# Batch 1's second product as seven block products, begun one stretch earlier

## The chip, the cores and the metric

The kernel runs on one core of one Trainium2 chip. A core has five engines that run side by side, each with its own queue of instructions in a fixed order: TensorE (PE, matrix products, results in PSUM), VectorE (DVE), ScalarE (ACT), GpSimd (POOL) and SyncE (SP, which here only issues transfers). An instruction starts when those ahead of it in its queue have been started and the semaphores that it waits for have been reached. The metric is the device time of one execution in microseconds (us); runs of the kernel before took 203.54 to 203.85 us, with a median of 203.78 over three.

## The reference

Two stages follow each other. Attention between 512 tokens and 32 state rows, for 8 batches b and 8 heads, and then a two-layer network over all rows:

```python
scores  = scale * x @ state.T        # 512 x 32 a head; softmax over the 32 -> a
xread   = a @ state                  # 512 rows a batch
scores2 = scale * state @ x.T        # 32 x 512; softmax over the 512 -> a2
sread   = a2 @ x                     # 32 rows a batch
y = concat(xread, sread)             # heads side by side: 544 rows of 512 a batch, 4352 in all
h = y @ w_in                         # 512 -> 2048
out = max(0.01 * h, h) @ w_out       # 2048 -> 512
```

Inputs and output are float32; the kernel computes its products in bfloat16 with float32 sums.

## The kernel before

**Stretches.** The work goes batch by batch. For batch b the kernel forms M = state @ w_in per head (`a_m` and `m_evict`, lines 359 to 385, in four column groups), the attention weights aT (256 rows of heads and states by 512 tokens), and then hT = leaky_relu(M.T @ aT), the hidden layer transposed: 16 tiles of 128 hidden columns by 512 tokens. A stretch is a loop of 16 steps s; step s makes tile s of hT with two products of 512 columns (`ff1`, line 389) into a PSUM bank of the tag `ph` (two banks in turn), from which ACT takes it with the leaky relu. In batch 1's stretch (the loop at line 1061) steps 6 and 10 make two tiles at once into the wide bank `big` (`ff1_pair`, line 399), and steps 7 and 11 make none. Between these steps other work is written by hand, on each engine in the order in which the code calls it: nothing is rearranged by a scheduler.

**The second product.** hT times w_out is done one batch behind. Two ways exist:
- plainly, in pieces (`piece`, line 593): piece (b, i, jq) adds four products of 512 columns for row group i (128 tokens) into a bank of the tag `py`, for a quarter jq of the hidden layer; after jq = 3 the bank is copied to `ysb` and stored.
- with seven block products instead of eight (Strassen's scheme in Winograd's form; `Fast`, line 638). Tokens and hidden columns are halved, and w_out is cut into four blocks B11 to B22. The operands of blocks 5, 6, 7 and 3 are sums: of hT's parts (`su0` to `su3`, DVE) and of w_out's (`tw`, four sums of 128 x 2048, made once by `weights_sum`). A block n goes in 8 units m; a unit is one product of 256 columns for each 128 tokens. Blocks run in the order 1, 2, 6, 5, 7, 3, 4 in two PSUM banks (`py`): when blocks 1, 6, 5 and 7 end, ACT copies the bank (`save`, `sv`); when 2, 3 and 4 end, DVE adds a saved copy (`join`) into `yo`, and POOL adds for block 7; then the result is stored.

Batches 2 to 7 use `Batch`: 512 tokens, so a unit is two products. Its first 15 units (`own`) run at the end of the batch's own stretch, as soon as the tiles of hT that they read are there; the other 41 in the next batch's. `PACE` says how many units each step runs. Batch 0 goes in pieces. Batch 1 is mixed: row groups 0 and 1 in pieces, of which 6 of 8 run in its own stretch (the list `fill`, odd steps 5 to 15) and two in steps 0 and 1 of batch 2's; row groups 2 and 3 as `Half`, a `Batch` of 256 tokens whose 56 units of one product run in batch 2's stretch, seven a step. `PACE2` is batch 2's own pace, used from step 10 on.

**Around it.** Batch 1's stretch also holds the last pieces of batch 0 (w_out's last quarter arrives at 34.75 us, so the pieces with jq = 3 are late: row groups 2 and 3 ahead of the loop, 0 and 1 in steps 1 and 3), batch 2's scores, their row maxima, the shift and the exponential (`a_scores`, `a_shift`, `a_exp`, `a_probs`; DVE, then ACT, then DVE), the column softmax (`a_max2`, `a_exp2`, and `a_probs2` for its factors), and the casts of batch 3's x (POOL). The sums of w_out are made in parts: half of two of them early on POOL, the rest on DVE ahead of the loop, the last one in batch 2's stretch at step 4.

## Time and profile before

| | |
|---|---|
| median of 3 runs (lowest, highest) | 203.78 us (203.54, 203.85) |
| the profiled execution, its span | 203.07 us, 201.3 us |
| busy share of PE, DVE, ACT, POOL | 96%, 78%, 72%, 24% |
| batch 1's stretch, 34.8 to 51.1 us | PE 16.2, DVE 13.7, ACT 13.6 us busy of 16.3 |
| batch 2's stretch, 51.1 to 73.6 us | PE 22.2, DVE 19.8, ACT 18.8 us busy of 22.5 |
| granted TensorE clock | 0.998 |

The profile is of one execution; times in it count from the span's start. A line of a timeline gives the start, the length, the engine, the line of the kernel, the operation, the tiles (written <- read) and their sizes, how many like it follow each other, and in brackets for how long the engine was idle before and what ended that. Lengths of PE's products overlap each other: what a product costs a busy PE is the distance from one start to the next. "The chain that ended last" follows the end of the program back through what each instruction waited for.

### The profile page before, as it was taken

The page shows a single profiled execution, that of the slowest core. Times are in us where ns is not written, and L with a number is a line of the kernel's source. Part 1 is how long each engine was busy: PE and PEld are TensorE (multiplying, and loading weights), DVE is VectorE, ACT ScalarE, POOL GpSimd, SP SyncE. Part 2 cuts the span into 40 slices and gives each one's busy share as a digit, 9 for nine tenths or more (in the row PEclk, how much of TensorE's full clock was granted, in tenths as well). Part 3 has the DMA queues.
Part 4 walks back from the last instruction along what each step waited for, and adds up shares of the span by engine and source line. Part 5 has one row for each costly group of instructions (what it writes and reads, how often), then busy time and mean ns, then how long its engine had stood idle before and what let it go on. Part 6 is the DMA issues. An engine that isn't in the chain of part 4 may idle for free.

```text
span 201.3 us, 4920 instructions
## 1 busy us (share of the span) xinstructions
PE 194.1 (96%) x2020; PEld 132.2 (66%) x2042; DVE 157.1 (78%) x242; ACT 145.3 (72%) x268; POOL 47.3 (24%) x76
## 2 busy tenths in 40 slices
PE   7899999999999999999999999999999999999993
PEld 2567633444377567766776677676766688799882
DVE  1676689798789889975997599779978977995622
ACT  3478747689869886978697868787878768767710
POOL 8841065040018004200420040200020014104250
PEclk9999999999999999999999999999999999999999
DMA  6999997999692993249433975250027101310035
GB/s 172 225 206 260 248 293 132 205 249 251 101 297 65 223 246 76 44 180 262 88 68 136 283 54 111 104 156 5 0 92 172 29 0 72 139 52 3 0 93 171
DMA packets 40758, 28.01 MB, mean 139 GB/s; under 512 B 25312, under 2 KB 37728, under 8 KB 40736
## 3 DMA queue, kind: packets, MB, share of 16 engines
q1 hardware_dynamic: 35536, 20.88, 43.0%
q0 software_dynamic: 4912, 6.55, 15.9%
q8 instruction: 16, 0.26, 0.5%
q10 hardware_dynamic: 288, 0.26, 0.5%
q14 instruction: 6, 0.05, 0.1%
HBM read 17.30 MB, written 8.91 MB: 130 GB/s over the span
## 4 chain that ended last, share of the span: by engine, by line
PE 80%; DMA 15%; POOL 2%; issue 1%; DVE 0%; POOLq 0%
PE yq L670 40%; PE ph L392 20%; DMA w_out_bf<-in_moe_w_out_dram 10%; DMA w_in_bf<-in_moe_w_in_dram 5%; PE py L599 4%; PE pf L466 3%; PE yu L670 3%; PE pm L371 3%; PE pl L555 2%; PE psn L337 1%; PE sc L211 1%; PE pyw L599 1%; PE phw L403 1%; POOL w_in_bf L123 1%; PE yz L670 0%
## 5 line engine op out<-in xcount | busy, mean ns | idle before, releaser
L397 ACT ACTIVATE hT<-ph 128x512 bf16<-128x512 f32 x100 | 58.9, 605 | 17.3 <-PE ph L392 13.1
L392 PE MATMUL ph<-aT,M 128*128 128x512 bf16 x183 | 54.9, 379 | 0.3
L670 PEld LDWEIGHTS <-su 128*128 128x128 bf16 x448 | 42.9, 98 | 13.8 <-DVE su L659 0.8
L670 PEld LDWEIGHTS <-hT 128*128 128x128 bf16 x312 | 30.1, 98 | 13.5 <-issue 2.0
L670 PE MATMUL yq<-tw_xf,su 128*128 128x256 bf16 x208 | 29.6, 273 | 0.3
L670 PE MATMUL yq<-w_out_bf,hT 128*128 128x256 bf16 x208 | 29.2, 273 | 0.1
L111 POOL CAST xb<-xl 128x512 bf16<-128x512 f32 (+1 forms) x24 | 14.3, 638 | 59.1 <-DMA xl<-in_x_dram 45.1
L392 PEld LDWEIGHTS <-M 128*128 128x128 bf16 x200 | 19.4, 98 | 7.2 <-issue 1.0
L659 DVE TENSOR_TENSOR su<-hT 128x1024 bf16<-128x1024 bf16 x26 | 17.9, 688 | 7.1 <-ACT hT L397 7.1
L740 POOL TENSOR_TENSOR yo<-sv,sv 128x512 f32<-128x512 f32 x6 | 7.8, 1302 | 41.0 <-ACT sv L679 25.4
L679 ACT COPY sv<-yq 128x512 f32<-128x512 f32 (+1 forms) x28 | 15.4, 554 | 2.1 <-PE yq L670 1.4
L599 PEld LDWEIGHTS <-hT 128*128 128x128 bf16 x96 | 9.0, 98 | 10.9 <-issue 1.3
L599 PE MATMUL py<-w_out_bf,hT 128*128 128x512 bf16 x60 | 15.4, 379 | 0.3 <-issue 0.2
L670 PE MATMUL yq<-tw_x,su 128*128 128x256 bf16 x104 | 14.6, 273 | 0.1
L670 PE MATMUL yq<-w_out_bf,su 128*128 128x256 bf16 x104 | 14.5, 273 | 0.2
L385 ACT CAST M<-pm 128x1024 bf16<-128x1024 f32 x13 | 13.2, 1014 | 0.9 <-PE pm L371 0.8
L670 PE MATMUL yq<-tw_x,hT 128*128 128x256 bf16 x96 | 13.6, 273 | 0.0
L682 DVE TENSOR_TENSOR yo<-yq,sv 128x512 f32<-128x512 f32 x17 | 11.6, 684 | 1.5 <-PE yq L670 1.5
L291 ACT ACTIVATE e<-sc,mcols 128x512 bf16<-128x512 f32 x16 | 11.0, 693 | 0.2 <-DVE mcols L285 0.2
L283 DVE TENSOR_REDUCE mcol<-sc 128x2 f32<-128x1024 f32 x8 | 9.7, 1216 | 0.0
L659 DVE TENSOR_TENSOR su<-su,hT 128x1024 bf16<-128x1024 bf16 x13 | 9.0, 692 | 0.4
L221 DVE TRANSPOSE_TENSOR_REDUCE mrow<-sc 128x32 f32<-128x1024 f32 x7 | 8.7, 1243 | 0.6 <-PE sc L211 0.5
(173 smaller groups left out, 299.0 us busy)
## 6 DMA issues: line engine op xcount, KB each, us to landing
xl<-in_x_dram SPq DMA_DIRECT2D x5, 1024.0 KB, 6.9
out_dram<-yo SPq DMA_DIRECT2D x10, 512.0 KB, 2.8
w_in_bf<-in_moe_w_in_dram POOLq DMA_DIRECT2D x4, 512.0 KB, 9.1
w_out_bf<-in_moe_w_out_dram POOLq DMA_DIRECT2D x4, 512.0 KB, 17.7
out_dram<-ysb SPq DMA_DIRECT2D x8, 256.0 KB, 5.7
xf<-in_x_dram SPq DMA_DIRECT2D x2, 512.0 KB, 5.1
x<-in_x_dram POOLq DMA_DIRECT2D x2, 512.0 KB, 14.1
xl<-in_x_dram POOLq DMA_DIRECT2D x1, 1024.0 KB, 20.4
```

Source lines behind the costliest of these rows:

```text
L111: copy(xs[b][:, :, h0:h1].rearrange("p t h d -> p h t d"), xl[b][:, h0:h1].rearrange("p h (t d) -> p h t d", t=NT),)
L221: nc.vector.tensor_reduce(out=m1[:], in_=flat.rearrange("p (c j) -> p c j", j=NS), axis=AX.X, op=ALU.max, apply_transpose=True,)
L283: nc.vector.tensor_reduce(out=m2[:], in_=a.sc[:], axis=AX.X, op=ALU.max, negate=True)
L291: nc.scalar.activation(out=a.e2[:, g], in_=a.sc[:, g, :], func=AF.Exp, bias=a.m2s[:, g:g + 1], scale=SCALE, accum_out=a.r2[:, g:g + 1],)
L385: copy(a.M[:, :, cols], pm[:])
L392: nc.tensor.matmul(ph[:], lhsT=a.M[:, g, P * j:P * (j + 1)], rhs=a.aT[:, g, :], start=(g == 0), stop=(g == 1),)
L397: nc.scalar.activation(out=hT[:, j, :], in_=ph[:], func=AF.Prelu, alpha=0.01)
L599: nc.tensor.matmul(y.py, lhsT=hT[:, j, P * i:P * (i + 1)], rhs=w_out_bf[:, j, :], start=(j == 0), stop=(j == 15),)
L659: (eng or nc.vector).tensor_tensor(out=S[n][:, ms], in0=u[:, ms], in1=v[:, ms], op=op)
L670: nc.tensor.matmul(bank[:, i, :], lhsT=lhs[:, m, P * i:P * (i + 1)], rhs=rhs[:, m, :], start=(first and m == 0 and (i == 0 or of is not No ...
L679: copy(t[:], bank)
L682: nc.vector.tensor_tensor(out=dst, in0=bank, in1=self.sv[n][:], op=ALU.add)
```

## The change

- `Half` goes. Batch 1's second product is a `Batch` of 512 tokens like the others, all seven blocks for all four row groups: 112 products of 256 columns in place of 32 of 512 and 56 of 256. Thirteen of its units run in batch 1's own stretch (`early`: 3 in step 7, then one or two a step), in an order of their own that follows the tiles of hT; 43 run in batch 2's stretch by a new `PACE2`, ahead of batch 2's 15 own ones.
- Batch 0's last pieces: only row group 2's stays ahead of the loop; row group 3's goes to step 1, 0's to step 3, 1's to step 5. The copy of row group 0's result moves from ACT to DVE.
- The sums of w_out on DVE come ahead of these copies; half of sum 0 and half of sum 3 move to POOL, ahead of its casts of batch 3's x; the other half of sum 3 comes in step 7 of batch 2's stretch.
- The factors of the column softmax (`a_probs2`) of batches 1, 2 and 3 are made together in step 11 of batch 2's stretch, behind which stands batch 1's last join; its buffer `r2` becomes three.
- In batch 2's stretch the first halves of the sums 0 and 1 come ahead of the copy of M, batch 3's scores go from step 1 to step 2, sums 2 and 3 stand in and behind the shift, the next batch's first sums go from step 12 to 13.
- On SP, batch 0's `a2T` transposition comes ahead of batch 0's four stores; batch 1's result leaves in two stores of 512 KB instead of four of 256 KB.

```diff
@@ -287,7 +287,7 @@
     def a_exp2(a, g):
         if g == 0:
             a.e2 = att.tile([P, 2, S], BF16, name="e2", tag="e2", bufs=3)
-            a.r2 = att.tile([P, 2], FP32, name="r2", tag="r2")
+            a.r2 = att.tile([P, 2], FP32, name="r2", tag="r2", bufs=3)
         nc.scalar.activation(
             out=a.e2[:, g], in_=a.sc[:, g, :], func=AF.Exp,
             bias=a.m2s[:, g:g + 1], scale=SCALE, accum_out=a.r2[:, g:g + 1],
@@ -691,7 +691,11 @@
             self.b, self.f = b, Fast(hT[:], 2 * P, [(spool, f"su{n}", 1) for n in range(4)], saved)
             self.units = [(n, m) for n in (1, 2, 6, 5, 7, 3, 4) for m in range(NM)]
             own = [(n, m) for n in (1, 2) for m in range(6)] + [(1, 6), (2, 6), (1, 7)]
-            assert len(own) == OWN
+            if b == 1:
+                own = [(n, 2 * c + m) for c in range(2) for n in (1, 2) for m in range(2)]
+                own += [(n, m) for m in (4, 5) for n in (1, 2)] + [(1, 6)]
+                self.units.sort(key=lambda u: u != (1, 7))
+            self.ahead = len(own)
             self.units = own + [u for u in self.units if u not in own]
             self.bank = {}
             self.yos = {}
@@ -749,25 +753,9 @@
                 f.join(self.yo(1)[:, :, :HC], bank, 7)
                 self.out(1)
 
-    class Half(Batch):
-
-
-        def __init__(self, hT):
-            super().__init__(1, hT)
-            self.f.__init__(hT[:, :, 2 * P:], P, self.f.homes, self.f.saved)
-            self.units = [(n, m) for n in (1, 2, 6, 5, 7, 3, 4) for m in range(NM)]
-
-        def yo(self, r):
-            if r not in self.yos:
-                self.yos[r] = ypool.tile([P, 1, DM], FP32, name="ysb", tag="ysb", bufs=3)
-            return self.yos[r]
-
-        def out(self, r, cols=slice(0, DM), i=None, eng=nc.sync):
-            eng.dma_start(rows_of(1)[2 + r], self.yo(r)[:, 0, :])
-
     OWN = 15
     PACE = (1, 4, 4, 4, 3, 4, 4, 3, 4, 4, 4, 4, 3, 4, 3, 3)
-    PACE2 = (0,) * 10 + (3, 3, 2, 2, 2, 3)
+    PACE2 = (1, 2, 1, 3, 4, 4, 4, 4, 4, 4, 4, 4, 4, 5, 5, 5)
 
     att_of = [Attn() for _ in range(B)]
     a0, a1, a2 = att_of[:3]
@@ -1043,38 +1031,43 @@
     a_probs(a1)
     for i in range(NT):
         piece(0, h0, i, 2)
-    for i in (2, 3):
-        piece(0, h0, i, 3, copy=None)
-    for i in (2, 3):
-        y_store(0, i, VEC)
+    piece(0, h0, 2, 3, copy=None)
+    for n in (2, 0, 1):
+        weights_sum(n, 4, 8)
+    weights_sum(3, 4, 8, nc.gpsimd)
+    weights_sum(0, 0, 4, nc.gpsimd)
     for h in range(0, H, 2):
         cast_x(3, h, h + 2, POO)
     a_a2t(a0)
-    weights_sum(2, 4, 8)
-    weights_sum(1, 4, 8)
-    weights_sum(0)
 
 
 
     h1 = hpool.tile([P, 16, S], BF16, name="hT", tag="hT")
-    fill = [(0, h0, 0, 3), (0, h0, 1, 3)] + [(1, h1, i, jq) for jq in range(3) for i in range(2)]
+    before = Batch(1, h1)
+    early = {7: 3, 8: 1, 9: 2, 10: 1, 11: 2, 12: 1, 13: 1, 14: 1, 15: 1}
+    assert sum(early.values()) == before.ahead
     for s in range(16):
         if s in (6, 10):
             ff1_pair(a1, h1, s, "big")
         elif s not in (7, 11):
             ff1(a1, h1, s)
-        if s % 2:
-            pb, hT, i, jq = fill[s // 2]
-            piece(pb, hT, i, jq)
+        if s == 1:
+            piece(0, h0, 3, 3, copy=None)
+            for i in (2, 3):
+                y_store(0, i, VEC)
+        elif s in (3, 5):
+            piece(0, h0, s // 2 - 1, 3, copy=VEC if s == 3 else SCA)
+        else:
+            before.run(early.get(s, 0))
         if s == 3:
             a_scores(a2)
             m_evict(a2, 0, a_m(a2, 0, "big"), SCA)
             a_shift(a2)
             a_max2(a2)
-            a_probs2(a0)
         if s == 7:
             a_exp(a2)
             a_probs(a2)
+            a_probs2(a0)
             a_open(att_of[3], 3)
             a_xt_dma(att_of[3])
         elif s in (9, 11):
@@ -1084,32 +1077,26 @@
 
 
 
-    a_probs2(a2)
     pm = [a_m(a2, 1, "big"), a_m(a2, 2, "sc")]
+    for n in (0, 1):
+        before.f.sums(n, 0, 4)
     m_evict(a2, 1, pm[0], VEC)
     m_evict(a2, 2, pm[1], SCA)
-    a_probs2(a1)
     a_a2t(a1)
 
 
 
-    before, half = None, Half(h1)
     for b in range(2, B):
         hT = hpool.tile([P, 16, S], BF16, name="hT", tag="hT")
         a = att_of[b]
         nxt = att_of[b + 1] if b + 1 < B else None
         now = Batch(b, hT)
-        std = []
-        if b == 2:
-            std = [(i, 3) for i in range(2)]
-            for n in (0, 1):
-                half.f.sums(n)
 
         def fill(s):
             units((PACE2 if b == 2 else PACE)[s])
 
         def units(n):
-            left = min(n, len(before.units)) if before else 0
+            left = min(n, len(before.units))
             if left:
                 before.run(left)
             if n > left:
@@ -1131,10 +1118,9 @@
                 if b + 2 < B:
                     load_x(b + 2, nc.sync)
                 a_a2t(a)
-                if before:
-                    for n in (0, 1):
-                        before.f.sums(n, 4, 8)
-            elif s == 1:
+                for n in (0, 1):
+                    before.f.sums(n, 4, 8)
+            elif s == (2 if b == 2 else 1):
                 if nxt is not None:
                     a_scores(nxt)
                 m_evict(a, 3, a_m(a, 3, "big"), SCA)
@@ -1143,20 +1129,23 @@
                 elif b % 2:
                     a_sread_rows([att_of[b - 2], att_of[b - 1]])
                 if b == 2:
-                    half.f.sums(2)
                     a_shift(nxt, 0)
+                    before.f.sums(2)
+                    a_shift(nxt, 1)
+                    a_max2(nxt)
+                    before.f.sums(3, 0, 4)
+                    before.f.sums(3, 4, 8)
                 elif nxt is not None:
                     a_shift(nxt)
                 if b + 2 < B:
                     open_xb(b + 2)
                     for h in range(0, H, 2):
                         cast_x(b + 2, h, h + 2, POO)
-                if before:
+                if b > 2:
                     before.f.sums(2, 4, 8)
-            elif s == 3:
-                if before:
-                    before.f.sums(3)
-                if nxt is not None and b > 2:
+            elif s == 3 and b > 2:
+                before.f.sums(3)
+                if nxt is not None:
                     a_max2(nxt)
             elif s == 4:
                 if b == 2:
@@ -1168,7 +1157,7 @@
             elif s == 8:
                 if nxt is None:
                     a_sread(a)
-            elif s == 12:
+            elif s == (13 if b == 2 else 12):
                 for n in range(3):
                     now.f.sums(n, 0, 4)
             if nxt is None:
@@ -1191,6 +1180,10 @@
                 if b == 2 and s < 11:
                     if s in (8, 9):
                         a_exp2(nxt, s - 8)
+                    elif s == 7:
+                        a_exp(nxt)
+                        weights_sum(3, 0, 4)
+                        a_probs(nxt, 0)
                 elif s == 5:
                     a_exp(nxt)
                 elif s in (7, 8):
@@ -1198,24 +1191,11 @@
                     if s == 7:
                         a_probs(nxt)
                 elif s == 11:
-                    a_probs2(nxt)
+                    for some in ((a1, a2, nxt) if b == 2 else (nxt,)):
+                        a_probs2(some)
                 elif s in (12, 13):
                     SCA(nxt.M[:, s - 12, DM:2 * DM], pm1[:, s - 12, :])
-            if std:
-                i, jq = std.pop(0)
-                piece(1, h1, i, jq)
-            elif b == 2 and half.units:
-                half.run(7)
-                if s == 4:
-                    a_shift(nxt, 1)
-                    half.f.sums(3)
-                    weights_sum(3)
-                    a_max2(nxt)
-                elif s == 6:
-                    a_exp(nxt)
-                elif s == 8:
-                    a_probs(nxt, 0)
-            elif s != 11 and not fast:
+            if s != 11 and not fast:
                 fill(s)
             if s == 10 and nxt is not None:
                 pm0 = a_m(nxt, 0, "big")
```

## The prediction

> **What bounds the kernel now.** I read the page's first part, then the chain that ended last, then the table by stretch for the two stretches that the change touches, then the timelines of TensorE (PE), ScalarE (ACT), VectorE (DVE) and GpSimd (POOL) there. The page and the chain:
>
> ```profile
> PE 194.1 (96%) x2020; PEld 132.2 (66%) x2042; DVE 157.1 (78%) x242; ACT 145.3 (72%) x268; POOL 47.3 (24%) x76
> ```
>
> ```profile
> 15.54 19.21 DMA w_out_bf<-in_moe_w_out_dram
> 34.80 1.24 PE pyw L599 x5
> ```
>
> From 34.80 us, when the last quarter of w_out has landed, the chain is PE's own work almost without a break; so in what follows time is PE's work plus PE's waits. By stretch (columns: length, busy time of each engine with instructions, granted clock, DMA):
>
> ```profile
> 34.80:51.10 16.30, 16.19 (x86) 7.00 (x87) 13.65 (x21) 13.62 (x26) 2.29 (x4) 1.00 1.07 223
> 51.10:73.60 22.50, 22.18 (x237) 13.73 (x242) 19.82 (x31) 18.80 (x36) 4.98 (x6) 1.00 0.79 184
> ```
>
> The first line is batch 1's stretch, the second batch 2's. The clock granted is 1.00. ACT and DVE are busy 13.6 of 16.3 us in the first: they follow PE closely there, and if PE's work shrinks by some 2 us, one of them can become the bound. PE's timeline (start, length, what, count) gives the prices:
>
> ```profile
> 40.07 0.41 PE L211 MATMUL sc<-xT,st_t 64*32 64x512 bf16 x8
> ...
> 51.12 0.63 PE L371 MATMUL pm<-w_in_bf,st_t 64*32 64x512 bf16 x16
> ...
> 52.12 1.03 PE L599 MATMUL py<-w_out_bf,hT 128*128 128x512 bf16 x4
> ...
> 74.22 1.05 PE L670 MATMUL yq<-tw_xf,su 128*128 128x256 bf16 x8
> ```
>
> Four 512-column products are issued in 0.86 us (the last one's end is modelled, so spacing counts, not length; 52.12 to 52.99 us), 0.2156 us each. Eight 256-column products take 0.87 us (0.109 each; the next instruction follows at 75.10). A group of scores and M products costs 0.56 (40.07 to 40.63), the pair of M products after the stretch also 0.56. DVE, ACT and POOL:
>
> ```profile
> 27.87 1.25 DVE L229 STREAM_TRANSPOSE mrowb<-mrow 128x1024 f32<-128x1024 f32 x1
> 29.15 1.22 DVE L234 TENSOR_TENSOR sh<-sc,mrowb 128x1024 f32<-128x1024 f32 x1
> ...
> 34.97 0.69 DVE L259 TENSOR_TENSOR aT<-e,qb 128x1024 bf16<-128x1024 bf16 x1
> ...
> 40.55 1.25 DVE L221 TRANSPOSE_TENSOR_REDUCE mrow<-sc 128x32 f32<-128x1024 f32 x1
> ...
> 84.63 1.05 DVE L259 TENSOR_TENSOR aT<-e,qb 128x1024 bf16<-128x1024 bf16 x1
> ```
>
> ```profile
> 44.44 1.06 ACT L241 ACTIVATE e<-sh 128x1024 bf16<-128x1024 f32 x1
> 45.40 1.06 ACT L397 ACTIVATE hT<-ph 128x512 bf16<-128x512 f32 x2
> 46.35 0.69 ACT L291 ACTIVATE e<-sc,mcols 128x512 bf16<-128x512 f32 x1
> ...
> 47.02 1.03 ACT L407 ACTIVATE hT<-phw 128x1024 bf16<-128x1024 f32 x1
> 47.92 0.70 ACT L291 ACTIVATE e<-sc,mcols 128x512 bf16<-128x512 f32 x1
> ...
> 48.58 1.11 ACT L397 ACTIVATE hT<-ph 128x512 bf16<-128x512 f32 x2
> ```
>
> ```profile
> 26.77 2.12 POOL L636 TENSOR_TENSOR tw_x<-w_out_bf 128x1024 bf16<-128x1024 bf16 x1 [10.47 <-DMA w_out_bf<-in_moe_w_out_dram]
> 28.96 2.13 POOL L636 TENSOR_TENSOR tw_xf<-w_out_bf,tw_x 128x1024 bf16<-128x1024 bf16 x1
> ...
> 43.28 2.29 POOL L111 CAST xb<-xl 128x512 bf16<-128x512 f32 x4 [9.36 <-DMA xl<-in_x_dram]
> ...
> 83.86 1.27 POOL L740 TENSOR_TENSOR yo<-sv,sv 128x512 f32<-128x512 f32 x1 [5.99 <-ACT sv L679]
> ```
>
> To be seen: DVE's shift of batch 2's scores begins at 40.55 and ACT's exponential of it at 44.44, 3.89 later; from there ACT runs without a hole to 49.7, and the relu after the second `e<-sc,mcols` starts 4.14 after the exponential. After the change ACT has these instructions in the same order.
>
> **PE's work.** Rows 0 and 1 of batch 1's second product go as 8 pieces of four 512-column products: 32 x 0.2156 = 6.90 us out. Rows 2 and 3 are 56 products of 256 columns, 6.10 us; now all four rows make 112, 12.21 us. Sum: 12.21 - 6.10 - 6.90 = -0.79 us. That is the whole gain that PE can have. In batch 1's stretch PE loses 24 of the 512s (one piece of batch 0 also moves into it from ahead of it, which is neutral) and gains 26 of the 256s: -5.17 + 2.83 = -2.34. Batch 2's stretch loses 8 of the 512s and 56 of the 256s and gains 86: -1.72 - 6.10 + 9.37 = +1.55. So the change moves work out of a stretch where ACT has 2.7 us to spare into one where PE is the only bound.
>
> **Batch 1's stretch, walked through.** PE: piece (0,2,3) from 34.80 to 35.66. The first step needs aT, which DVE writes until 35.66 (34.97 + 0.69); signal and weight load add about 0.14 (nowhere shown alone; bounds 0 and the 0.31 of a switch to small tiles, 40.07 less 39.76), so 35.80. Two steps of 0.43 and a piece to 37.52, two steps and piece (0,0,3) to 39.25; scores at about 39.35 instead of 40.07. DVE: three sums of w_out fit from 35.6 to 37.5 while PE works; two copies follow; the copy that was ACT's can begin when (0,0,3) has left PE, about 39.46, and holds DVE for 0.60. So the shift starts at 40.06, though its scores are there at 39.80: the moved copy takes 0.26 from the 0.72 gained. ACT's exponential: 40.06 + 3.89 = 43.95.
>
> PE meanwhile: 39.35 + 0.56 = 39.91, steps 4 and 5 with piece (0,1,3) to 41.63, wide step 6 to 42.50, then with 3, 1, 2, 1, 2, 1 units (0.218 each) steps 7 to 12 end at 46.84. Step 13's unit (1,5) reads hT column 10, which the wide relu writes: in the rows above it starts 2.58 after the exponential and takes 1.02, so 47.55, with signal and weight load 47.70; PE is there at 47.27 and waits 0.43. Step 14 needs the `ph` bank that step 12's relu frees: 43.95 + 4.14 + 0.60 = 48.69, about 48.73; PE is there at 47.92 and waits 0.81. Then 48.73 + 0.65 + 0.65 = 50.03, with the switch of tiles 50.12 for the M products instead of 51.12. The stretch gains 1.00 of its 2.34.
>
> Behind it: ACT has the 1.01 us M copy, a relu and the copy of block 1 in line, and batch 2's third step waits for the first relu's bank about 0.17 (PE there at 52.20, relu ended 52.33 plus 0.04). Before lost 0.12 in this stretch (68.91 to 69.03), which the fuller steps now cover.
>
> **The moves that cost nothing, and their cover.** POOL's two sums (2.12 each, 37.5 to 41.8) stand ahead of its casts, which waited for the load of x until 43.28: 1.5 us of cover. If it were gone, the casts, batch 3's xT and its scores would be late next; xT is issued at 45.6 as before. SP: batch 0's a2T now goes ahead of four 256 KB stores, two of which left earlier; nobody waits for stores, the state loads and xT behind them stand behind the cast anyway. Later two 512 KB stores replace two 256 KB ones and the two pieces' ones; batch 2's first join into the same buffer comes near 73.3, some 8 us after batch 1's store goes (a store lands in 2.8). DVE in batch 2's stretch: two more sums (1.20), one sum twice as wide (0.53), one more sum (0.61), three joins wider by 0.26 (0.78), two of the three statistics pairs come in from elsewhere (0.65), half of the last w_out sum goes (1.62 to 0.61): +2.8 us or so, against 2.7 idle (22.5 less 19.8) and 1.55 of added length. The tightest: block 3's first sum ends near 60.9, PE wants it near 62.0; its cover is 1.1 us. ACT there: two copies of 0.59 and four of 0.37 become four of 0.58, about even. Joins ahead of batch 2's sums: the last join is ready when PE ends block 4, so it delays those sums by at most its 0.60, and before batch 3's step 2 they have over 3 us.
>
> **Sum.** -0.79 + 0.14 + 0.43 + 0.81 + 0.17 - 0.12 = +0.64 us. Rounding and reading of the signal times move this by 0.15 or so; I take +0.6. The profiled execution took 203.07 us (span 201.3 and 1.8 around it); it becomes about 203.7. The median of the three runs is 203.78, 0.7 above the profiled one; on it the forecast is **204.4 us**, 0.3% slower. What this kernel's measurement can tell from no change is about 0.2%, 0.41 us.
>
> **Where a page bears on it.** The row: aT on DVE took 1.05 us at 84.63 beside a POOL add, 0.69 at 34.97 alone. The Trainium skill, "SBUF — State Buffer", section "SBUF: two separate sides", says that VectorE and GpSimd take a shared port pair as an exclusive lock and the later one "fully blocks", for a VectorE instruction with two SBUF inputs or in a two-port mode. By that rule POOL's new sums hold none of the copies and the shift, which have one SBUF input at most, and the trace agrees (27.87 and 29.15 took 1.25 and 1.22 us beside POOL's sums of 26.77 and 28.96); a lock without that condition would give the last rival.
>
> **Rivals.** (1) *ACT's debt never reaches PE, and it gets faster.* If the exponential starts early enough, PE's two waits go. Each 0.1 us of an earlier start takes 0.1 off the waits; from 43.3 on the change breaks even, at about 42.7 both are gone and the sum is near -0.6, 203.2; with the full -0.79, 203.0. For it: PE reaches the scores 0.72 earlier, and nothing in the trace of before shows PE waiting for ACT there. Against: DVE's chain of 3.89 is serial. (2) *The waits and the saving cancel:* the exponential starts near 43.4; 203.8, no change. (3) *Batch 2's stretch also waits on DVE:* from 1.1 us of lateness on, block 3 waits for its sum. DVE's +2.8 against 4.2 of room argues against it; the casts of x on POOL beside the wide sum argue for it (59.60: four took 3.73 instead of 2.29). A sum held as long as those casts (1.44) and by one cast more (0.61), less the 1.1 of cover, gives 0.9 more: 205.3. (4) *POOL's sums hold DVE's copies and shift:* each can be held up to 2.12, so up to 2.1 more on the exponential, one for one: 206 at most. The rows at 27.87 and 29.15 speak against it; a copy of PSUM beside a POOL sum is not in the trace (bounds 0 and 2.12; I take 0, the two neighbours' value).
>
> **Numbers.** Forecast 0.51 (its own range 204.0 to 204.9), rival 1 0.20, rival 2 0.12, rival 3 0.13, rival 4 0.04. Faster by over 0.2%: 0.20. Within 0.2% (203.37 to 204.19): rival 2 and the low tail of the forecast, 0.24. Slower: 0.56. The range from 203.0 to 205.3 leaves out rival 4, the tail of rival 3 and a little under rival 1.
>
> **What will show it.** Right if: no PE wait before the scores (near 39.35), the exponential near 43.95, PE waiting for ACT between 47 and 49 by 1.0 to 1.4 us in two places, the M products near 50.1, and `psn` of batch 3's stretch near 74.2 instead of 73.58. The forecast is wrong if the exponential starts before 43.3, if PE waits for DVE's `su` in batch 2's stretch, or if DVE's copies near 37.7 take over 0.9 us beside POOL.

## The result and the profile after

The changed kernel takes 204.2 us (median of eight runs, 203.74 to 204.63); the kernel before took 203.72 us on the same chip (203.53 to 203.98). The ratio is 1.0026, with a 95% interval of 1.0014 to 1.0037: slower by about 0.53 us, where the forecast was 204.4 us and a loss of 0.6. The profiled execution took 204.26 us, span 202.5; it was forecast at 203.7.

The page's first part, then the table by stretch for the two stretches (columns as before: length, busy time of PE, its weight loads, DVE, ACT, POOL, granted clock, DMA):

```profile
PE 195.2 (96%) x2066; PEld 134.3 (66%) x2066; DVE 159.9 (79%) x246; ACT 144.9 (72%) x265; POOL 51.2 (25%) x78
```

```profile
34.80:50.20 15.40, 14.35 (x91) 7.02 (x89) 14.46 (x21) 12.49 (x24) 6.48 (x6) 1.00 1.06 231
50.20:74.20 24.00, 23.99 (x254) 15.92 (x260) 22.49 (x36) 19.26 (x36) 4.57 (x6) 1.00 0.63 161
```

PE's share is 96% as before, but batch 1's stretch now has holes: 14.35 us busy of 15.4, where before it was 16.19 of 16.3. Batch 2's stretch has hardly any (23.99 of 24.0), and DVE fills 22.49 us of it (19.82 of 22.5 before). PE's timeline:

```profile
36.29 1.04 PE L392 MATMUL ph<-aT,M 128*128 128x512 bf16 x4
...
39.85 0.41 PE L211 MATMUL sc<-xT,st_t 64*32 64x512 bf16 x8
...
47.35 0.59 PE L392 MATMUL ph<-aT,M 128*128 128x512 bf16 x2
48.11 0.39 PE L670 MATMUL yq<-w_out_bf,hT 128*128 128x256 bf16 x2 [0.16 <-ACT hT L407]
49.26 0.59 PE L392 MATMUL ph<-aT,M 128*128 128x512 bf16 x2 [0.76 <-ACT hT L397]
...
50.65 0.63 PE L371 MATMUL pm<-w_in_bf,st_t 64*32 64x512 bf16 x16
...
52.30 0.60 PE L670 MATMUL yq<-w_out_bf,hT 128*128 128x256 bf16 x4
52.91 0.59 PE L392 MATMUL ph<-aT,M 128*128 128x512 bf16 x2
...
64.88 0.84 PE L371 MATMUL pm<-w_in_bf,st_t 64*32 64x512 bf16 x24
...
66.54 1.03 PE L392 MATMUL ph<-aT,M 128*128 128x512 bf16 x4
...
74.58 0.70 PE L337 MATMUL psn<-xb,a2T 128*32 128x64 bf16 x64
```

Step 13 begins at 47.35, and its unit is due 0.43 later, at 47.78; it starts at 48.11, 0.33 late. Step 14 is due 0.22 behind that unit, at 48.33, and starts at 49.26, 0.93 late. (The bracket, here 0.16 and 0.76, holds only what the profile puts down to the semaphore; it comes out 0.17 below the lateness counted this way.) Together 1.26 us. In batch 2's third step four products from 52.30 on end their issue at 52.74, and the step starts at 52.91: 0.17. ACT, DVE and POOL in the same stretch:

```profile
44.44 1.06 ACT L241 ACTIVATE e<-sh 128x1024 bf16<-128x1024 f32 x1 [0.21 <-DVE sh L234]
...
47.02 1.03 ACT L407 ACTIVATE hT<-phw 128x1024 bf16<-128x1024 f32 x1
...
48.58 1.11 ACT L397 ACTIVATE hT<-ph 128x512 bf16<-128x512 f32 x2
```

```profile
35.54 0.69 DVE L259 TENSOR_TENSOR aT<-e,qb 128x1024 bf16<-128x1024 bf16 x1
...
38.23 1.29 DVE L609 COPY ysb<-pyw 128x512 f32<-128x512 f32 x2 [0.19 <-PE pyw L599]
39.96 0.69 DVE L609 COPY ysb<-py 128x512 f32<-128x512 f32 x1 [0.44 <-PE py L599]
40.56 1.24 DVE L221 TRANSPOSE_TENSOR_REDUCE mrow<-sc 128x32 f32<-128x1024 f32 x1
...
64.73 0.18 DVE L250 TENSOR_SCALAR r<-r 128x32 f32<-128x32 f32 x1
...
65.78 0.69 DVE L1205 CAST M<-pm 128x512 bf16<-128x512 f32 x1
```

```profile
38.12 2.12 POOL L636 TENSOR_TENSOR tw_x<-tw_xf,w_out_bf 128x1024 bf16<-128x1024 bf16 x1 [3.97 <-DVE tw_xf L636]
40.20 2.12 POOL L636 TENSOR_TENSOR tw_xf<-w_out_bf 128x1024 bf16<-128x1024 bf16 x1
43.70 2.28 POOL L111 CAST xb<-xl 128x512 bf16<-128x512 f32 x4 [1.38 <-DMA xl<-in_x_dram]
```

The exponential starts at 44.44, 3.88 behind the maximum at 40.56, which had to wait for the moved copy (39.96). The wide relu starts 2.58 and the relu of step 12 4.14 behind the exponential, as before. The copies on DVE beside POOL's sum took 0.69 and, two together, 1.29 us; POOL's sums ended at 42.3, and its casts still waited 1.38 us for x. Everything in this execution is about half a microsecond later than forecast from the first step on, and the chain that ended last says why: it no longer starts with w_out's landing, but with the first load of x and DVE's work on batch 1's weights.

```profile
1.26 6.25 DMA xf<-in_x_dram
...
34.26 1.26 DVE qb L258
```

`aT` began at 35.54 here and at 34.97 in the profile of before. There it did not matter, as the first step came 0.86 after aT's end at 35.66; here the first step starts 0.06 after aT's end. The first step and batch 3's `psn` in the profile of before:

```profile
36.52 1.03 PE L392 MATMUL ph<-aT,M 128*128 128x512 bf16 x4
...
73.58 0.70 PE L337 MATMUL psn<-xb,a2T 128*32 128x64 bf16 x64
```

### The profile page after: what moved, and what is told of

The parts are those of the page before. It is cut to its first block, busy times and chain, and to the rows that moved or that the text cites. A ratio compares the mean times of both kernels' runs of the same rounds, so it can differ in the third digit from the quotient of the medians.

```text
span 202.5 us, 4991 instructions
## 1 busy us (share of the span) xinstructions
PE 195.2 (96%) x2066; PEld 134.3 (66%) x2066; DVE 159.9 (79%) x246; ACT 144.9 (72%) x265; POOL 51.2 (25%) x78
## 4 chain that ended last, share of the span: by engine, by line
PE 83%; DVE 8%; DMA 3%; ACT 3%; issue 0%; POOL 0%; SPq 0%; DVEq 0%; ACTq 0%; POOLq 0%
PE yq L670 41%; PE ph L392 20%; PE pm L371 4%; DMA xf<-in_x_dram 3%; PE pf L466 3%; PE yu L670 3%; PE ph L944 2%; PE pl L555 2%; PE py L599 1%; PE pyw L599 1%; DVE mrowb L229 1%; DVE sh L234 1%; DVE mrow L221 1%; PE sc L211 1%; PE psn L337 1%; ACT hT L397 1%
## 5 line engine op out<-in xcount | busy, mean ns | idle before, releaser
L392 PE MATMUL ph<-aT,M 128*128 128x512 bf16 x200 | 58.2, 379 | 0.9 <-ACT hT L397 0.8
L670 PEld LDWEIGHTS <-su 128*128 128x128 bf16 x480 | 45.9, 98 | 15.0 <-DVE su L659 0.8
L670 PEld LDWEIGHTS <-hT 128*128 128x128 bf16 x336 | 32.3, 98 | 15.4 <-issue 2.1
L670 PE MATMUL yq<-w_out_bf,hT 128*128 128x256 bf16 x224 | 31.7, 273 | 0.2 <-ACT hT L407 0.2
L670 PE MATMUL yq<-tw_xf,su 128*128 128x256 bf16 x224 | 31.7, 273 | 0.0
L111 POOL CAST xb<-xl 128x512 bf16<-128x512 f32 (+1 forms) x24 | 12.8, 578 | 50.2 <-DMA xl<-in_x_dram 50.2
L659 DVE TENSOR_TENSOR su<-hT 128x1024 bf16<-128x1024 bf16 (+1 forms) x27 | 18.9, 701 | 7.6 <-ACT hT L397 7.6
L744 POOL TENSOR_TENSOR yo<-sv,sv 128x512 f32<-128x512 f32 x7 | 9.1, 1295 | 42.9 <-issue 21.5
L679 ACT COPY sv<-yq 128x512 f32<-128x512 f32 x28 | 16.3, 586 | 3.0 <-PE yq L670 2.5
L682 DVE TENSOR_TENSOR yo<-yq,sv 128x512 f32<-128x512 f32 x20 | 13.6, 682 | 1.5 <-PE yq L670 1.5
L659 DVE TENSOR_TENSOR su<-hT,su 128x2048 bf16<-128x2048 bf16 (+1 forms) x8 | 9.4, 1187 | 0.0
```

What stands on the lines that cost most here:

```text
L111: copy(xs[b][:, :, h0:h1].rearrange("p t h d -> p h t d"), xl[b][:, h0:h1].rearrange("p h (t d) -> p h t d", t=NT),)
L392: nc.tensor.matmul(ph[:], lhsT=a.M[:, g, P * j:P * (j + 1)], rhs=a.aT[:, g, :], start=(g == 0), stop=(g == 1),)
L659: (eng or nc.vector).tensor_tensor(out=S[n][:, ms], in0=u[:, ms], in1=v[:, ms], op=op)
L670: nc.tensor.matmul(bank[:, i, :], lhsT=lhs[:, m, P * i:P * (i + 1)], rhs=rhs[:, m, :], start=(first and m == 0 and (i == 0 or of is not No ...
L679: copy(t[:], bank)
L682: nc.vector.tensor_tensor(out=dst, in0=bank, in1=self.sv[n][:], op=ALU.add)
```

## The experiments

All ratios are to the kernel before, run on the same chip in the same rounds. The experiments ran on three chips, and the changed kernel itself was timed only in the first set of runs, so a difference between an experiment and the changed kernel is a difference of two ratios, uncertain by 0.3 to 0.4 us; where it is smaller, the profiles have to decide. Because the first step comes at a different time in each execution (35.52 to 36.64 below), two profiles are best compared by distances inside them: from the scores of batch 2 to the M products behind batch 1's stretch (S to M: what PE's waits cost there), and from these to batch 3's `psn` (M to psn: batch 2's stretch). In every profile the first step and the scores are 3.54 to 3.56 apart.

| kernel | ratio (95%) | first step | S to M | M to psn |
|---|---|---|---|---|
| before | 1 | 36.52 | 11.05 | 22.46 |
| changed | 1.0026 (1.0014 to 1.0037) | 36.29 | 10.80 | 23.93 |
| exponentials later | 1.0021 (1.0005 to 1.0037) | 35.93 | 10.13 | 24.13 |
| copy back on ACT | 1.0015 (1.0005 to 1.0024) | 35.78 | 10.57 | 23.93 |
| both | 1.0007 (0.9992 to 1.0022) | 35.60 | 10.01 | 24.77 |
| POOL's sums late | 1.0026 (1.0014 to 1.0039) | 35.99 | 10.80 | 24.10 |
| M copy on ACT | 1.0029 (1.0017 to 1.0040) | 36.14 | 10.79 | 23.98 |
| both, M copy on ACT | 0.9991 (0.9982 to 1.0000) | 35.52 | 10.01 | 23.98 |
| both, w_out sum early | 0.9982 (0.9973 to 0.9991) | 35.81 | 10.01 | 23.93 |
| both, M copy and sum | 0.9993 (0.9984 to 1.0002) | 35.81 | 10.02 | 23.97 |
| changed, DVE 0.6 more | 1.0047 (1.0034 to 1.0061) | 36.10 | 10.80 | 23.93 |
| before, DVE 0.6 more | 0.9999 (0.9989 to 1.0010) | 36.64 | 11.06 | 22.70 |
| changed, POOL's sums on DVE | 1.0044 (1.0031 to 1.0057) | 35.92 | 11.32 | 23.92 |
| changed, ACT 0.5 more | 1.0042 (1.0028 to 1.0056) | 35.85 | 11.31 | 23.93 |

### The column exponentials two steps later

```diff
-        elif s in (9, 11):
-            a_exp2(a2, s // 2 - 4)
+        elif s in (11, 13):
+            a_exp2(a2, int(s == 13))
```

> The changed kernel with the two 0.70 us column exponentials of batch 2 issued two steps later (steps 11 and 13 instead of 9 and 11); nothing else moves. Theory A (my prediction: ScalarE's line behind batch 2's exponential is what PE waits for in steps 13 and 14): the wide relu and the relu of step 12 come 0.70 earlier each, so PE's wait for hT of 0.16 to 0.33 goes and its wait of 0.8 to 0.9 for the bank falls to 0.2 or less; the M products come 0.6 to 0.7 earlier, and the time is 0.6 to 0.7 below that of the changed kernel (204.2), near 203.55, 0.1 to 0.2 below the kernel before. Theory B (the loss lies in batch 2's stretch, on VectorE's sums): the waits of batch 1's stretch fall, and as much comes back as a wait for su later; the time stays near 204.2. Theory C (the loss is the late first step, exposed to the arrival of x): the time stays within 0.1 of 204.2, because the waits in steps 13 and 14 only absorb that lateness.

Measured: 1.0021, twelve runs from 202.90 to 204.29 us. From the scores to the M products the stretch is 0.67 shorter, as theory A had it, but by the median little arrives at the end. PE and DVE of this kernel:

```profile
48.22 0.59 PE L392 MATMUL ph<-aT,M 128*128 128x512 bf16 x2 [0.42 <-ACT hT L397]
...
65.50 0.38 PE L392 MATMUL ph<-aT,M 128*128 128x512 bf16 x1
66.14 0.59 PE L392 MATMUL ph<-aT,M 128*128 128x512 bf16 x2 [0.26 <-DVE M L1205]
```

```profile
65.40 0.68 DVE L1205 CAST M<-pm 128x512 bf16<-128x512 f32 x1
```

The unit of step 13 no longer waits, and step 14, due at 47.64, is 0.58 late in place of 0.93. But a wait has come up that neither A nor B had named. Step 11 of batch 2's stretch runs at 65.50 (the record of its second product is missing), and step 12, due at 65.93, starts at 66.14: it needs the bank from which DVE copies a part of batch 3's M, and DVE ends that copy at 66.08. In the changed kernel the copy started at 65.78 (0.90 behind the M products at 64.88, as soon as they are done) and ended at 66.47; steps 11 and 12 ran on without a hole from 66.54, so step 12 came at 66.97. With the 0.06 from the copy's end to the step, the cover was about 0.45 us: less than the 0.67 by which this kernel brings PE there earlier, and the 0.21 that is missing is what PE waits. (The expectation of the M copy on ACT, below, takes step 11 for the step that needs the bank.) So theory A is right on where the loss arises and wrong on what is won by taking it away; B is right that a part comes back later, on DVE, but not at a sum `su`. In this profile, of an execution of 203.47 us, only 0.20 of the 0.67 comes back; what the executions near 204.3 lost no trace shows.

### Row 0's copy back on ACT

```diff
-            piece(0, h0, s // 2 - 1, 3, copy=VEC if s == 3 else SCA)
+            piece(0, h0, s // 2 - 1, 3, copy=SCA)
```

> The changed kernel with row 0's copy of batch 0's output given back to ScalarE; all else as changed. Theory A (VectorE holds back the shift of batch 2's scores by this copy, 0.26, and the shift sets ScalarE's exponential): the shift starts 0.26 earlier behind the scores, the exponential too, PE's two waits fall by 0.26 together, and the time is about 0.26 below the changed kernel, near 203.95; ScalarE has 2.7 us to spare ahead of its exponential, so the copy costs it nothing. Theory B (the copy is hidden, or ScalarE's copy delays a relu that PE waits for): no change to 0.1, 204.2. Theory C (VectorE's copies are held by Pool's sums of w_out, so the copy costs far more than 0.60): a gain of over 0.5.

Measured: 1.0015, by the middle of the intervals 0.22 us less than the changed kernel's 1.0026; the intervals overlap, so the time alone would not tell this from nothing. DVE:

```profile
39.82 1.25 DVE L221 TRANSPOSE_TENSOR_REDUCE mrow<-sc 128x32 f32<-128x1024 f32 x1 [0.81 <-PE sc L211]
```

DVE's maximum started 0.48 behind the scores here (39.82 and 39.34) and 0.71 in the changed kernel, and from the scores to the M products it is 0.23 shorter. Theory A, with its number in the profile.

### Both edits

The two diffs above together.

> The changed kernel with both edits: the two column exponentials two steps later and row 0's copy back on ScalarE. Theory A: with both, ScalarE's line is 0.96 ahead of where it was for the bank of step 14, both waits of PE go, and the time is 0.7 to 0.75 below the changed kernel, near 203.5, 0.2 below the kernel before; that is less than the sum of the two edits, since no more than the wait is there to be saved, and it is what is left of the 0.79 of PE's saved work after the 0.14 and the 0.17 of the other two waits. Theory B (a later wait takes its place, on VectorE's sums or in batch 2's first steps): no better than the exponentials moved alone, or worse.

Measured: 1.0007, runs from 202.75 to 204.16 us. In the profile, of an execution of 203.63 us, S to M falls by 0.79 to 10.01, but M to psn grows by 0.84: theory B, in the place that the first run above had shown. The median is 0.39 us below the changed kernel's by the middle of the intervals, which overlap. PE, DVE and POOL of this kernel:

```profile
47.78 0.59 PE L392 MATMUL ph<-aT,M 128*128 128x512 bf16 x2 [0.31 <-ACT hT L397]
...
63.40 0.84 PE L371 MATMUL pm<-w_in_bf,st_t 64*32 64x512 bf16 x24
...
66.34 0.59 PE L392 MATMUL ph<-aT,M 128*128 128x512 bf16 x2 [0.90 <-DVE M L1205]
```

```profile
61.36 1.09 DVE L636 TENSOR_TENSOR tw_x<-tw_xf,w_out_bf 128x1024 bf16<-128x1024 bf16 x1
...
63.65 1.11 DVE L250 TENSOR_SCALAR r<-r 128x32 f32<-128x32 f32 x1
...
65.61 0.68 DVE L1205 CAST M<-pm 128x512 bf16<-128x512 f32 x1
```

```profile
59.20 3.73 POOL L111 CAST xb<-xl 128x512 bf16<-128x512 f32 x4 [13.90 <-DMA xl<-in_x_dram]
...
63.45 1.27 POOL L744 TENSOR_TENSOR yo<-sv,sv 128x512 f32<-128x512 f32 x1
```

Step 12 (66.34) waits 0.9 for DVE's copy of M (`DVE M L1205`). The M products start at 63.40, so the copy could start at 64.30; DVE comes to it at 65.61. From batch 2's aT at 47.82 on, DVE has no hole in which to catch up, and on the way it is held by POOL. The tensor-scalar at 63.65 took 1.11 us, where it takes 0.18 in the changed kernel's profile (64.73): it ends at 64.76, 0.04 after POOL's add (63.45 + 1.27) ends. The half sum of w_out at 61.36 took 1.09 in place of 0.68 (62.86 there), and POOL's four casts beside such sums took 3.73 in place of 2.29 (59.10 there). The transposing sum beside POOL keeps its 1.23 (62.38 here, 63.47 there). The Trainium skill, "SBUF — State Buffer", section "SBUF: two separate sides", says just this: of a GpSimd instruction and a VectorE one with two SBUF inputs or in a two-port mode, whichever starts first holds the shared port pair for its whole instruction. The sums' rows agree with it; that the tensor-scalar runs in such a mode no run shows by itself, but its row ends as if it did.

### POOL's sums behind its casts

```diff
-    weights_sum(3, 4, 8, nc.gpsimd)
-    weights_sum(0, 0, 4, nc.gpsimd)
     for h in range(0, H, 2):
         cast_x(3, h, h + 2, POO)
+    weights_sum(3, 4, 8, nc.gpsimd)
+    weights_sum(0, 0, 4, nc.gpsimd)
```

> The changed kernel with Pool's two sums of w_out (2.12 us each) issued behind its casts of batch 3's x instead of ahead of them. Theory A (the sums touch nobody: they end 1.5 us before x lands, and VectorE's copies beside them take what they take without them): no change, within 0.15 of 204.2. Theory B (Pool's sums hold VectorE's copies of PSUM and the shift beside them, my last rival): the copies and the shift come sooner, the exponential with them, and the time falls by 0.3 or more. Theory C (the sums delay the casts): batch 3's cast starts as x lands, and any gain would be seen in batch 3's transposes, not in batch 1's stretch.

Measured: 1.0026, the same as the changed kernel; S to M the same to 0.01. DVE and POOL:

```profile
37.93 1.29 DVE L609 COPY ysb<-pyw 128x512 f32<-128x512 f32 x2 [0.19 <-PE pyw L599]
39.66 0.69 DVE L609 COPY ysb<-py 128x512 f32<-128x512 f32 x1 [0.44 <-PE py L599]
...
46.92 0.92 DVE L250 TENSOR_SCALAR r<-r 128x32 f32<-128x32 f32 x1
...
49.54 0.89 DVE L259 TENSOR_TENSOR aT<-e,qb 128x1024 bf16<-128x1024 bf16 x1
```

```profile
45.68 2.12 POOL L636 TENSOR_TENSOR tw_x<-tw_xf,w_out_bf 128x1024 bf16<-128x1024 bf16 x1
```

Without a POOL sum beside them the copies at 37.93 and 39.66 take 1.29 and 0.69, to the digit what they took with one. So theory A, and the last rival is out. Moved to 45.68, the sums now do hold DVE: the tensor-scalar at 46.92 takes 0.92 for 0.18, aT 0.89 for 0.69, DVE reaches the first sum of batch 2's stretch 1.0 later behind the exponential (50.62 and 44.14, before the move 49.94 and 44.44), and PE waits 0.19 for the M copy, which shows as 0.17 in M to psn. Where POOL's work stands costs nothing in itself; beside which of DVE's instructions it stands does.

### Relieving DVE in batch 2's stretch

What follows was to tell whether the M copy is really the second limit: it is moved to ACT in batch 2's stretch (in the changed kernel and in the one with both edits), or DVE's line ahead of it is made shorter by one half sum of w_out, or both.

```diff
-                for g, copy in enumerate((VEC, SCA)):
+                for g, copy in enumerate((SCA if b == 2 else VEC, SCA)):
```

```diff
-    for n in (2, 0, 1):
+    for n in (2, 0):
         weights_sum(n, 4, 8)
+    weights_sum(3, 0, 4)
+    weights_sum(1, 4, 8)
...
                         a_exp(nxt)
-                        weights_sum(3, 0, 4)
                         a_probs(nxt, 0)
```

> The changed kernel with one copy moved: in batch 2's stretch the first of the two M copies behind step 10 goes on ScalarE instead of VectorE. Theory A (formed from the first runs: VectorE has no hole from batch 1's aT to this copy, and the copy is the next thing that PE waits for once batch 1's stretch gets faster): in the changed kernel's profile the copy ended at 66.47 and PE was due at 66.52, so here almost nothing changes, 0 to 0.2 us faster on the average of the executions; ratio to the kernel before 1.0015 to 1.0026. Theory B (ScalarE's line is the only bound, in this stretch too): 0.58 more on ScalarE makes it slower by 0.2 or more, ratio 1.0035.

> The changed kernel with the two column exponentials two steps later, row 0's copy back on ScalarE, and the M copy behind step 10 of batch 2's stretch on ScalarE. Theory A: the 0.9 us wait for VectorE's copy of M goes, and the time comes to 0.2 to 0.3 below the kernel before (ratio 0.9985 to 0.999), with executions closer together than the 1.4 us of the version without this copy moved, since what varied was how VectorE's line met Pool's casts. Theory B (another wait behind it takes the same time, on VectorE's aT or its sums): the ratio stays near 1.0007 and the spread stays.

> The changed kernel with the two column exponentials later, row 0's copy on ScalarE, and the last half sum of w_out (0.69 alone, 1.09 in the last profile) taken out of VectorE's line in batch 2's stretch and put ahead of the copies of rows 2 and 3, where VectorE had 0.8 us idle ahead of batch 2's maximum. Theory A (length of VectorE's line sets the M copy): the wait of 0.9 falls by 0.7 to 1.1 to near 0, ratio 0.9985 to 0.9995. Theory B (not the length, but the meeting with Pool's casts and add): the line is shorter but meets Pool elsewhere; executions stay spread over more than 1 us and the ratio falls by less than 0.0005.

> Both: the M copy on ScalarE and the last half sum of w_out early, with the exponentials later and row 0's copy on ScalarE. Theory A: nothing more is there to gain than with one of them, ratio 0.9985 to 0.999, since what is left of PE's waits is 0.31 in step 14, the late first step and batch 2's third step. Theory B (VectorE's line is waited for at a second place too): better than either alone by 0.2 or more, 0.998.

Measured: on the changed kernel the copy alone brings nothing (1.0029; the distances are within 0.05 of the changed kernel's, as the cover of 0.45 there would have it; the interval holds B's 1.0035 too, but nothing in the trace got slower). With both edits it brings 0.9991, runs from 202.71 to 203.38 us, and M to psn is back at 23.98. The half sum early brings 0.9982, runs from 202.70 to 203.31: 0.37 us faster than the kernel before, and the best of all. Both together: 0.9993. The three intervals overlap and the three profiles agree to 0.05 us, so they are not told apart; theory A holds. DVE and PE of the kernel with the sum early:

```profile
36.88 0.69 DVE L636 TENSOR_TENSOR tw_x<-tw_xf,w_out_bf 128x1024 bf16<-128x1024 bf16 x1
...
39.85 1.25 DVE L221 TRANSPOSE_TENSOR_REDUCE mrow<-sc 128x32 f32<-128x1024 f32 x1 [0.49 <-PE sc L211]
...
64.52 0.69 DVE L1206 CAST M<-pm 128x512 bf16<-128x512 f32 x1
```

```profile
47.99 0.59 PE L392 MATMUL ph<-aT,M 128*128 128x512 bf16 x2 [0.31 <-ACT hT L397]
...
63.61 0.84 PE L371 MATMUL pm<-w_in_bf,st_t 64*32 64x512 bf16 x24
...
65.27 1.03 PE L392 MATMUL ph<-aT,M 128*128 128x512 bf16 x3
```

The half sum (36.88) stands where DVE would have waited for the scores; the maximum still begins 0.48 behind them. The M copy starts at 64.52, 0.91 behind the M products: DVE is on time again, and PE goes through steps 11 and 12 from 65.27 on without a hole. This although the tensor-scalar was held here as well (62.85, 0.70 us). What is left of PE's waits in batch 1's stretch is step 14's: due at 47.52, it starts at 47.99, 0.47 late (0.31 by the bracket).

### The slack of the first step

```diff
+    nc.vector.tensor_reduce(out=spare[:], in_=idle[:], axis=AX.X, op=ALU.max)
     a_probs(a1)
```

> The changed kernel with one VectorE instruction more, a maximum over 512 columns (about 0.6 us by the half sums' 0.68 of twice the columns and the shift of the maximum's 1.21 for 1024), ahead of batch 1's row sums, so that aT comes that much later. Nothing else changes. Theory A (the piece that was moved behind the first step was the slack of that step: the kernel before had 0.86 us between the end of aT and the first step, the changed one has none): the whole 0.6 to 0.7 comes out at the end, ratio to the kernel before near 1.006. Theory B (ScalarE's waits of 1.2 us in steps 13 and 14 are set by VectorE's chain behind the scores, which has slack ahead of its maximum, and absorb a late first step): no more than 0.2 above the changed kernel, 1.0035 or less.

> The kernel before with the same VectorE instruction ahead of batch 1's row sums. Theory A: its first step has 0.86 us of slack behind aT, VectorE 1.06 idle ahead of the two copies that follow, so nothing is lost: ratio 1.000, at most 1.001. Theory B (VectorE's line is waited for in the kernel before too, at batch 2's scores or later): 0.3 us or more, ratio 1.0015 or above.

Measured: 1.0047 with the change and 0.9999 without it. The kernel before, DVE and then PE, and PE of the changed kernel:

```profile
35.78 0.69 DVE L260 TENSOR_TENSOR aT<-e,qb 128x1024 bf16<-128x1024 bf16 x1
```

```profile
36.64 1.03 PE L393 MATMUL ph<-aT,M 128*128 128x512 bf16 x4
```

```profile
36.10 1.04 PE L393 MATMUL ph<-aT,M 128*128 128x512 bf16 x3 [0.28 <-DVE aT L260]
```

The added instruction holds DVE for 0.60 us (31.86 to the next start at 32.46). In the kernel before aT then ends at 36.47, the first step starts 0.12 later than in its profile, and nothing of it is left in the ratio. (Its M to psn is 0.24 longer than in the profile of before. That lies in the M products of step 10 alone, 66.15 to 67.18 for 66.04 to 66.81, ahead of which DVE's tensor-scalar beside POOL's casts took 0.58 for 0.44 and its sum 0.87 for 0.70; the trace puts the hole down to nothing.) In the changed kernel the ratio grows by 0.0021, 0.43 us (0.06 to 0.8, the two intervals taken together): less than A's 0.6 to 0.7 by its middle, more than B's 0.2, and neither is outside. Inside the profile both distances are unchanged (10.80 and 23.93), and PE waits for aT at the first step, so what it costs lies ahead of the scores, as A says.

### More on ACT, and POOL's sums on DVE

```diff
             ff1(a1, h1, s)
+        if s == 8:
+            SCA(idle[:], idle[:])
```

```diff
-    weights_sum(3, 4, 8, nc.gpsimd)
-    weights_sum(0, 0, 4, nc.gpsimd)
+    weights_sum(3, 4, 8)
+    weights_sum(0, 0, 4)
```

> The changed kernel with one ScalarE copy more (128x512, 0.5 to 0.6 us) in step 8 of batch 1's stretch, behind the exponential. Theory A (ScalarE's line is what PE waits for in steps 13 and 14): one for one, PE's waits there go from 0.92 to about 1.4 by the profile's waits, the time 0.45 to 0.55 above the changed kernel, ratio 1.0048 to 1.0053. Theory B (VectorE's line to the M copy in batch 2's stretch sets the end, and batch 1's stretch has slack to it): less than 0.2 above, 1.0035 or less.

> The changed kernel with Pool's two sums of w_out given back to VectorE in the same place (2 x 0.6 us more on VectorE ahead of the copies). Theory A (VectorE's chain to the exponential has 0.19 and 0.44 us of idle time ahead of its copies, the rest of the 1.2 delays it): the exponential 0.5 to 0.6 later, PE's waits in steps 13 and 14 longer by as much, ratio 1.0045 to 1.0055. Theory B (Pool's sums hold VectorE by as much as they take from it): no change, 1.0026.

Measured: 1.0042 and 1.0044. These two and the run with more DVE work are from one chip, on which the changed kernel itself was not timed; on the two other chips kernels much like it (POOL's sums late, the M copy on ACT) came to 1.0026 and 1.0029. In the first, PE:

```profile
48.18 0.39 PE L670 MATMUL yq<-w_out_bf,hT 128*128 128x256 bf16 x2 [0.68 <-ACT hT L407]
```

In the second, PE and ACT:

```profile
40.25 0.41 PE L371 MATMUL pm<-w_in_bf,st_t 64*32 64x512 bf16 x8 [0.36 <-DVE ysb L609]
```

```profile
44.59 1.06 ACT L241 ACTIVATE e<-sh 128x1024 bf16<-128x1024 f32 x1 [0.17 <-DVE sh L234]
```

With the ACT copy the wait in step 13 grew by 0.52, that of step 14 is the same behind it (0.76 at 49.33); S to M grows by 0.51 for an ACT copy of 0.51 (45.43 to the next start at 45.94): one for one inside the stretch. The time grew by 0.33, with an interval that holds A's number and B's; the trace decides for A. With POOL's sums on DVE the exponential came 5.11 behind the scores in place of 4.59 (44.59 and 39.48, 44.44 and 39.85), and S to M grew by 0.52. That is A's delay, but not at A's place: steps 13 and 14 are 1.23 us late together, against 1.26 in the changed kernel, and PE pays the whole of it earlier, at the M products of step 3 (40.25), which wait for DVE's delayed copies and start 0.54 behind their time.

## Why the prediction came out

The time and the sign were right, and nearly all of it for the reasons given; the one step that was wrong did not show in the time of the changed kernel itself.

- **PE's work, -0.79.** Borne out by the distances: S to M 10.80 against the forecast's 10.77 (39.35 to 50.12). M to psn was forecast at 24.08 and came to 23.93; that is 0.15 less, and the kernel before had a hole of 0.16 without a releaser in that stretch (its piece at 54.65) that is gone with the piece.
- **First step, +0.14 behind PE's piece, set by aT.** From aT's end to the first product it was 0.06, inside the bounds (the upper one, 0.31, holds the 0.22 of a product besides the switch). What the step missed is that it gave away the 0.86 us by which aT could come late. In all twelve profiles of kernels with the change the first step starts 0.06 behind aT's end; in the eleven of them without the added DVE instruction that lay between 35.52 and 36.29. The pair of runs with more DVE work shows that a late aT now costs time and before did not.
- **The moved copy, 0.26.** 0.23 in distance; the time agrees (0.22) but does not tell it from nothing.
- **PE's waits, 0.43 and 0.81.** 0.33 and 0.93, together 1.26 for 1.24; that ACT's line makes them is shown by taking from it (0.67 off), by adding to it (0.51 on), and by the copy.
- **Batch 2's third step, 0.17.** 0.17.
- **POOL's sums, nothing.** Shown by the run with them late; on DVE instead they would have cost 0.52 us by the profile, 0.37 by the medians.
- **The tightest cover in batch 2's stretch, 1.1 us at block 3's sum.** This is the step that failed. DVE did not lack time for that sum: it ended at 61.93, PE read it from 62.61 on, 0.68 later, and waited for it in no profile. But the copy of M behind step 10 had only about 0.45 us of cover, and the prediction did not walk DVE's line that far. It summed DVE's added work (2.8; the table has 22.49 for 19.82, 2.7) against idle time and added length over the whole stretch. Ahead of the M copy itself the kernel before had 2.2 us of idle time (13.62 busy of 15.84, 51.10 to 66.94), and the changed kernel has 0.4 left (15.16 of 15.58, 50.20 to 65.78), all of it between instructions that follow each other without a wait. So the third rival named the right engine and the wrong instruction. In the changed kernel ACT's waits hide this; as soon as they are shortened by more than the cover, it takes over.
- **Not foreseen at all:** from psn to the end of the span the profiles of all kernels with the change have 127.9 us (127.90 to 127.96), the two of kernels without it 127.7 (127.72 and 127.69). PE's last product comes exactly as much later as psn (1.00 us, 197.78 and 196.78), and in all fourteen profiles the last DMA packet ends 126.1 behind psn, so the 0.2 lies behind the last transfer. The traces show where 0.12 of it comes from. At its end the program has SP wait for the semaphores of the DMA one after the other, 0.06 us apart, always in the same order. In the two kernels without the change the last store signals semaphore 115, in all twelve with it 105, which stands two places ahead: two more waits follow the landing. The rest lies between the last packet and its landing (0.49 and 0.52 without the change, 0.59 to 0.63 with it), and its cause is open. No run was made on either. The 0.2 is about as large as what batch 2's stretch came out shorter, so the sum is right in part by luck: two misses cancel.

The two profiles differ by 1.2 us in span, the medians by 0.5. That of before is faster (203.07 us) than any of its eight timed runs, and that of after has the latest first step of the eleven. With ACT's wait cut to 0.47 us and DVE's gone, the same products are 0.18% faster than the kernel before (0.09% to 0.27%), 0.37 us. Between the two profiles the span differs by 0.08 (201.30 and 201.22), and the terms give that: of the 0.79, step 14 takes 0.47, the end 0.2, batch 2's third step 0.17 and the first step 0.15 (it comes 0.71 earlier for a piece of 0.86), and the two holes of before that are gone (0.12 and 0.16) give 0.28. The other 0.29 no trace shows: the profiled execution of before (203.07) is 0.17 below its median on that chip, and that of the faster kernel (202.99) 0.07 above its own. Whether the same edits would help the kernel before was not tried; its PE had no wait in batch 1's stretch to be taken away.

## What to carry to other kernels

Work moved from a stretch where PE's helpers have room into one where they have little can be paid for twice: its old stretch shrinks only until the next engine's line bounds it (here ACT's, 1.26 us), and in its new one every helper's line must be walked to each instruction that PE waits for, not summed over the stretch (here DVE's, 0.45 us of cover). When a wait is taken away, look in the trace for the instruction with the least cover behind it before counting the gain. And a piece of work that stands between a late arrival and its first use is slack: whoever moves it away gives every later jitter a way into the time.

## What the runs showed of the hardware

- A DVE tensor-scalar on 128 x 32 float32 took 0.18 us alone, and 0.55 to 1.11 us beside a POOL add or sum, ending with it; a sum of two SBUF operands of 128 x 1024 bfloat16 took 0.68 alone and up to 1.09 beside POOL's casts, and four casts 2.28 to 3.73. Copies of PSUM (0.69, two together 1.29), transposes (1.25) and transposing reductions (1.23) beside POOL kept their times.
- The kernels in which DVE's line was the bound and met POOL (exponentials later, both) spread over 1.4 us from run to run; with row 0's copy back on ACT, on the same chip, the spread was 0.6, and in those in which DVE's line was relieved, on another chip, 0.6 to 0.7. That the meeting makes the spread is argued from single profiles, not shown run by run.
- SP's closing waits for the DMA semaphores stand 0.06 us apart in these traces, so which semaphore the last store signals moved the end by 0.12 us (115 or 105, told above).
